# Attention and two feed-forward networks on one core: ten of sixteen probability transfers issued from GpSimd instead of eight, and another order of ten steps of the second network

## The chip, the cores and the metric

The kernel runs on one core of a Trainium2 chip. The metric is the device time of one execution in microseconds; the time before is a median of three runs.

## The reference, cut to what matters

Attention comes first, over 4 batches, 8 heads, 576 positions and 64 dimensions a head. The scores get a bias that a small network makes from the positions:

```python
scores = scale * np.matmul(q, k.transpose(0, 1, 3, 2))
...
h = np.maximum(x @ w1 + b1, 0.0)          # x: log distance of the pair of positions, over log position
bias = h @ w2
attn = np.exp(scores + bias - max) / (sum + 1e-09)
attn_out = attn @ v                        # 2304 tokens x 512
x = (sigmoid(x @ w_gate) * (x @ w_val)) @ moe_w_out        # 512 -> 1536 -> 512
h = x @ w_in                                               # 512 -> 2048
out = (h * clip(h + 3, 0, 6) / 6) @ moe2_w_out             # 2048 -> 512
```

Everything is in 32-bit floats. The kernel keeps that accuracy by splitting each operand of the large products into a high and a low part and multiplying three times (high by high, high by low, low by high).

## The kernel before, in words

**Blocks.** The 576 positions are cut into five chunks: four of 128 and one of 64 (`QC`). A chunk of all four batches is 512 tokens (256 in the last). Chunk 0 gets its attention in a lead-in. Then come five blocks: block k runs both feed-forward networks on chunk k, and between the steps of the networks the attention of chunk k + 1. Blocks begin in the profile at about 81, 311, 557, 783 and 987 us.

**Steps.** The networks of a block are 68 steps, listed by `moe_steps` (line 41). Each takes one weight tile of 512x128 and makes one 128-row product: 24 steps G and V (gate and value), 12 steps Y (first network's output, three for each of four output tiles o), then 16 steps H (second network's hidden tiles) and 16 steps O (its output). Eight O steps, groups g of 0 and 1, stand after the tenth H; the last eight, groups 2 and 3, stand at the end, positions 60 to 67: for each o first g = 2, then g = 3. Group g reads the hidden tiles 4g to 4g + 3, so g = 3 needs the last H (position 59).

**One step.** `product` (line 644) issues twelve matmuls: for each of four input tiles c, three products of high and low parts. They add up in one PSUM bank, `ps`. Then ScalarE and VectorE take the bank: after an H the lines 704, 705, 676 and 678 (clip, product, high part `gh`, low part `gl`), after the last Y of an o the lines 676 and 680 (`xyh`, `xyl`, the inputs of the H steps), after the last O line 720 and the store of line 729. In the last block, of 256 columns, the Y and O steps with o below 3 are "wide": eight matmuls of line 655 in place of twelve, and two more instructions afterwards (670, 671).

**Banks.** The small products draw on a pool of four PSUM banks, `mm_ps`: each step's `ps`, the two tails of `pair_qk` (line 510), the output of `pair_av` (line 567), and the bias products of line 171 that are made "apart".

**Attention between the steps.** `block_events` gives each piece of attention a position on the scale of the 68 steps, and `block` runs all pieces that are due ahead of a step. In blocks 1 to 3 a pair of units goes through `pair_qk` (scores, line 524), `pair_soft` (minimum, exponential, normalisation), `att_turn` (VectorE transposes in 32x32 blocks into the tile `t`, line 446) and `pair_turn` (line 451): sixteen transfers of 72 KB from `t` to `pT`, which finish the transposition. `pair_av` (line 477) multiplies `pT` by the values. `t` and `pT` have one buffer each: the transfers of a pair wait until `pair_av` of the pair before has read `pT`, and the transposes of the next pair wait until all sixteen have read `t`. In block 1 a pair is due every 5.1 steps, in block 2 every 8.1. The sixteen transfers are issued from two queues (lines 454 to 459):

```python
        for i in range(4):
            for q in range(4):
                (nc.sync if p[0][0] < 4 and i > 1 else nc.gpsimd).dma_start(
```

**Order of the work.** TensorE's order is the program's in all blocks. In blocks 1 to 4 the order of the instructions on VectorE, ScalarE, GpSimd and SyncE is laid out by a planner, which works from its own costs of the instructions. Weight tiles come from HBM, five steps ahead, into six buffers (`w_load`, line 586), from SyncE. A queue's instructions run in order.

Of the kernel before, what the change touches and what calls it, by code (L numbers as in the profile page):

```python
# [36 lines left out]
YG, OG = 3, 2  # L37
# [3 lines left out]
def moe_steps():  # L41

    seq = []
    for f in range(NF1):
        seq += [("G", f), ("V", f)]
    for o in range(4):
        seq += [("Y", g, o) for g in range(NF1 // 4)]
    for f in range(NF2):
        seq += [("H", f)]
        if f == NF2 // 2 + 1:  # L50
            seq += [("O", g, o) for o in range(4) for g in range(2)]
    seq += [("O", g, o) for o in range(4) for g in range(2, 4)]
    return seq


STEPS = moe_steps()
NSTEP = len(STEPS)
assert NSTEP == 3 * NF1 + 2 * NF2
# [3 lines left out]
def fused_kernel(ctx: ExitStack, tc: tile.TileContext, qd, kd, vd, tz, td, cst, iden, wpack, out):  # L62
    nc = tc.nc
# [21 lines left out]
    def mm_ps():  # L85
        return m1.tile([128, 512], F32, name="ps")
# [22 lines left out]
    ps = mm_ps()  # L109
# [6 lines left out]
    ps = mm_ps()  # L116
# [334 lines left out]
    def pair_turn(p):  # L451

        t, pt = tn_q.pop(0), A["pt"].tile([128, 4, 2, 9, 32], F32, name="pT")
        for i in range(4):
            for q in range(4):
                (nc.sync if p[0][0] < 4 and i > 1 else nc.gpsimd).dma_start(  # L456
                    out=pt[32 * q:32 * q + 32, i].rearrange("j u t i -> j (u t i)"),
                    in_=t[32 * i:32 * i + 32, q].rearrange("j u t i -> j (u t i)"),
                )
        for x, u in enumerate(p):  # L460
            st[u]["pt"] = pt[:, :, x]
# [89 lines left out]
    def pair_soft(p, x):  # L551
        u = p[x]
        d = st[u]
        ps, m = d.pop("ps"), d["m"]
        for h in range(2):
            pair_min(u, h, ps[:, h, 0:NT], 0, NT, m[:, h:h + 1], 2 + h)
        d["m"] = m[:, 2:4]
        att_exp(u)
        att_norm(u)
        if u[0] == 1:  # L560
            return
        att_turn(p, x)
        if x:
            pair_turn(p)
# [8 lines left out]
    wq, wf_q = {}, {}  # L573
# [67 lines left out]

    ys, gs, accs, th_q, ps_q = {}, {}, {}, {}, {}

    def product(n, nt, ops, mm_ps, first=True, last=True, wide=False):
        wp = wq.pop(n)
        wh, wl = wp[:, 0], wp[:, 1]
        if first:
            ps_q[0] = mm_ps()
        ps = ps_q[0]
        for c in range(4):  # L650
            xh, xl, *both = ops[c]
            if wide:
                pair = [(wh, both[0], ps[:, 0:2 * nt]), (wl, xh, ps[:, 0:nt])]
                for w, x, o in pair if c == 0 else pair[::-1]:
                    nc.tensor.matmul(  # L655
                        out=o, lhsT=w[:, c, :], rhs=x,
                        start=(first and c == 0 and w is wh), stop=(last and c == 3 and w is wh),
                    )
                continue
            for i, (w, x) in enumerate(((wh, xh), (wh, xl), (wl, xh))):  # L660
                nc.tensor.matmul(  # L661
                    out=ps[:, 0:nt], lhsT=w[:, c, :], rhs=x[:, 0:nt],
                    start=(first and c == 0 and i == 0), stop=(last and c == 3 and i == 2),
                )
        return whole(ps, nt) if wide and last else ps[:, 0:nt]

    def whole(ps, nt):

        lo = P["tmp"].tile([128, NTOK], F32, name="tmp")[:, 0:nt]
        nc.scalar.activation(out=lo, in_=ps[:, nt:2 * nt], func=AF.Copy)  # L670
        nc.vector.tensor_tensor(out=lo, in0=ps[:, 0:nt], in1=lo, op=ALU.add)
        return lo

    def split(p, nt, src, scale, nh, nl):
        hi, lo, *both = pair_tiles(p, nt, nh, nl)
        nc.scalar.activation(out=hi, in_=src, func=AF.Copy, scale=scale)  # L676
        if scale == 1.0:
            nc.vector.tensor_tensor(out=lo, in0=src, in1=hi.bitcast(F32), op=ALU.subtract)  # L678
        else:
            nc.vector.scalar_tensor_tensor(  # L680
                out=lo, in0=src, scalar=scale, in1=hi.bitcast(F32), op0=ALU.mult, op1=ALU.subtract
            )
        return hi, lo, *both

    def moe_step(k, i, P, mm_ps):
        n = k * NSTEP + i
        kind = STEPS[i]
        i0, qn = QC[k]
        nt = B * qn
        wide = 2 * nt <= NTOK  # L690
        if kind[0] in "GV":
            ps = product(n, nt, [xs[k, c] for c in range(4)], mm_ps, wide=wide)
            if kind[0] == "G":
                th = ps if wide else P["tmp"].tile([128, NTOK], F32, name="tmp")[:, 0:nt]
                nc.scalar.activation(out=th, in_=ps, func=AF.Tanh, scale=0.5)
                th_q[0] = th
            else:
                th = th_q.pop(0)
                nc.vector.scalar_tensor_tensor(out=th, in0=th, scalar=1.0, in1=ps, op0=ALU.add, op1=ALU.mult)  # L699
                gs[kind[1]] = split(P["gu"], nt, th, 1.0, "gh", "gl")  # L700
        elif kind[0] == "H":
            ps = product(n, nt, [ys[c] for c in range(4)], mm_ps)
            t = P["tmp"].tile([128, NTOK], F32, name="tmp")[:, 0:nt]
            nc.scalar.activation(out=t, in_=ps, func=AF.Relu, bias=3.0)  # L704
            nc.vector.scalar_tensor_tensor(out=t, in0=t, scalar=6.0, in1=ps, op0=ALU.min, op1=ALU.mult)  # L705
            gs[kind[1]] = split(P["gu"], nt, t, 1.0, "gh", "gl")
        elif kind[0] == "Y":
            _, g, o = kind
            ps = product(n, nt, [gs[4 * g + c] for c in range(4)], mm_ps, g == 0, g == YG - 1, wide and o < 3)
            if g == YG - 1:  # L710
                ys[o] = split(xy_p, nt, ps, 0.5, "xyh", "xyl")
        else:
            _, g, o = kind
            ps = product(n, nt, [gs[4 * g + c] for c in range(4)], mm_ps, g % OG == 0, g % OG == OG - 1, wide and o < 3)
            if g == OG - 1:
                accs[o] = P["acc"].tile([128, NTOK], F32, name="acc")[:, 0:nt]
                nc.scalar.activation(out=accs[o], in_=ps, func=AF.Copy, scale=1.0 / 6.0)
            elif g == 2 * OG - 1:
                a = accs.pop(o)
                nc.vector.scalar_tensor_tensor(  # L720
                    out=a, in0=ps, scalar=1.0 / 6.0, in1=a, op0=ALU.mult, op1=ALU.add
                )
                av = a.rearrange("p (b i) -> p b i", b=B)
                for ih in range(NH):
                    lo, hi = max(i0, ih * NI), min(i0 + qn, ih * NI + NI)
                    if lo < hi:
                        for x in range(2):
                            q = nc.gpsimd if k + 1 < NC else (nc.sync, nc.scalar)[x]
                            q.dma_start(  # L729
                                out=out[2 * ih + x, o, :, :, lo - ih * NI:hi - ih * NI],  # L730
                                in_=av[:, 2 * x:2 * x + 2, lo - i0:hi - i0],
                            )
# [242 lines left out]
    def block(k):  # L975
        ev = block_events(k)
        for i in range(NSTEP):
            while ev and ev[0][0] <= i:
                ev.pop(0)[1]()
            if k == 0 and i == NSTEP - 6:  # L980
                held.extend((issued[1], issued[2]))
            n = k * NSTEP + i
            if k == 0:
                if 10 <= n + WA + 1 < NSTEP:
                    w_load(n + WA + 1)
                for x in range(WB - 1 if i == 0 else WB, WB + 1):
                    w_store(n + x - 1)
                    w_split(n + x)
                if i == 0:
                    for last in issued[1], issued[2]:  # L990
                        ctx.enter_context(tc.issue_after(last.ins))
            if n + WA >= NSTEP:
                w_load(n + WA)
            moe_step(k, i, P, mm_ps)
        for e in ev:
            e[1]()
# [72 lines left out]
```

## Time and profile before

| | |
|---|---|
| median of 3 runs | 1091.34 us (1090.79 to 1093.15) |
| the profiled execution | 1092.8 us, its span 1091.0 us |
| TensorE (PE) busy | 99% of the span, 7042 matmuls |
| VectorE (DVE), ScalarE (ACT), GpSimd (POOL) busy | 59%, 49%, 12% |
| granted TensorE clock | 0.999 |
| DMA | 321.94 MB, mean 295 GB/s |

The profile is one execution. A row of the timeline is: start, duration, engine, line, operation, what it writes and reads, how many; in brackets, the idle time of the engine just before it and what ended that.

### The profile page before, as it was taken

The page shows a single profiled execution, that of the slowest core. Times are in us where ns is not written, and L with a number is a line of the kernel's source. Part 1 is how long each engine was busy: PE and PEld are TensorE (multiplying, and loading weights), DVE is VectorE, ACT ScalarE, POOL GpSimd, SP SyncE. Part 2 cuts the span into 40 slices and gives each one's busy share as a digit, 9 for nine tenths or more (in the row PEclk, how much of TensorE's full clock was granted, in tenths as well). Part 3 has the DMA queues.
Part 4 walks back from the last instruction along what each step waited for, and adds up shares of the span by engine and source line. Part 5 has one row for each costly group of instructions (what it writes and reads, how often), then busy time and mean ns, then how long its engine had stood idle before and what let it go on. Part 6 is the DMA issues. An engine that isn't in the chain of part 4 may idle for free.

```text
span 1091.0 us, 19679 instructions
## 1 busy us (share of the span) xinstructions
PE 1079.8 (99%) x7042; PEld 878.7 (81%) x7042; DVE 644.2 (59%) x1528; ACT 537.3 (49%) x1068; POOL 132.3 (12%) x253
## 2 busy tenths in 40 slices
PE   8999999999999999999999999999999999999998
PEld 4777788888887778788788788788788888888897
DVE  8888787797863457796745654656242416154433
ACT  8888688788953344564423342533032214223332
POOL 2000000000010011121311111111430202031000
PEclk9999999999999999999999999999999999999999
DMA  7977899999996789989998888797896969688997
GB/s 244 379 262 289 318 410 368 351 343 403 335 362 229 247 284 291 299 269 284 314 337 262 273 262 270 239 287 249 274 292 213 298 209 278 215 250 308 372 368 266
DMA packets 118480, 321.94 MB, mean 295 GB/s; under 512 B 20720, under 2 KB 29424, under 8 KB 118384
## 3 DMA queue, kind: packets, MB, share of 16 engines
q1 hardware_dynamic: 107968, 297.09, 78.6%
q0 software_dynamic: 9184, 23.25, 7.7%
q8 instruction: 56, 0.92, 0.3%
q10 hardware_dynamic: 1232, 0.35, 0.1%
q14 instruction: 40, 0.33, 0.1%
HBM read 245.08 MB, written 51.37 MB: 272 GB/s over the span
## 4 chain that ended last, share of the span: by engine, by line
PE 82%; ACT 7%; DMA 6%; DVE 3%; issue 2%; SPq 0%; POOL 0%; ACTq 0%; DVEq 0%; POOLq 0%
PE ps L661 59%; PE ps L477 7%; PE ps L655 6%; PE ps L524 3%; PE ps L359 2%; PE ps L416 2%; DMA wd<-wpack 1%; DMA wsp<-wp 1%; PE ps L171 1%; DMA vt<-vd 1%; ACT wp L603 1%; ACT s L390 1%; ACT z L156 1%; PE ps L179 1%; PE ps L530 1%
## 5 line engine op out<-in xcount | busy, mean ns | idle before, releaser
L661 PE MATMUL ps<-xyh,wp 128*128 128x512 f32 (+1 forms) x1472 | 428.7, 378 | 1.1 <-ACT wp L603 0.8
L661 PEld LDWEIGHTS ps<-xyh,wp 128*128 128x128 f32 x1472 | 263.3, 188 | 59.9 <-issue 2.8
L661 PE MATMUL ps<-gh,wp 128*128 128x512 f32 (+1 forms) x980 | 294.7, 383 | 0.5 <-ACT gh L676 0.5
L661 PE MATMUL ps<-xyl,wp 128*128 128x512 f32 x640 | 249.5, 390 | 0.3 <-DVE xyl L680 0.3
L661 PEld LDWEIGHTS ps<-gh,wp 128*128 128x128 f32 x980 | 178.7, 188 | 38.7 <-issue 3.1
L661 PE MATMUL ps<-gl,wp 128*128 128x512 f32 x448 | 174.8, 390 | 0.8 <-DVE gl L678 0.8
L456 POOL DMA_DIRECT2D pT<-t x192 | 94.4, 500 | 493.0 <-DVE t L446 152.8
L676 ACT ACTIVATE gh<-tmp 128x512 fp32r<-128x512 f32 (+1 forms) x140 | 82.1, 588 | 127.4 <-DVE tmp L699 84.0
L661 PEld LDWEIGHTS ps<-xyl,wp 128*128 128x128 f32 x640 | 120.2, 188 | 24.7 <-DVE xyl L680 0.8
L390 ACT ACTIVATE s<-s,m 128x576 f32<-128x576 f32 x144 | 110.3, 768 | 34.5 <-DVE m L546 34.0
L678 DVE TENSOR_TENSOR gl<-tmp,gh 128x512 fp32r<-128x512 f32 x112 | 76.5, 687 | 39.4 <-ACT gh L676 38.4
L661 PEld LDWEIGHTS ps<-gl,wp 128*128 128x128 f32 x448 | 84.1, 188 | 18.7 <-DVE gl L678 2.1
L477 PEld LDWEIGHTS ps<-pT,vt 128*64 128x64 f32 x1600 | 79.0, 137 | 13.0 <-issue 10.9
L477 PE MATMUL ps<-pT,vt 128*64 128x128 f32 (+1 forms) x1600 | 89.1, 265 | 0.1
L705 DVE SCALAR_TENSOR_TENSOR tmp<-tmp,ps 128x512 f32<-128x512 f32 (+1 forms) x80 | 50.0, 629 | 53.6 <-ACT tmp L704 52.2
L699 DVE SCALAR_TENSOR_TENSOR tmp<-tmp,ps 128x512 f32<-128x512 f32 x48 | 32.7, 682 | 74.2 <-PE ps L661 73.4
L704 ACT ACTIVATE tmp<-ps 128x512 f32<-128x512 f32 (+1 forms) x80 | 43.9, 549 | 43.4 <-PE ps L661 43.3
L403 DVE TENSOR_SCALAR s<-s,r 128x576 f32<-128x576 f32 x128 | 61.4, 516 | 1.7
L502 ACT ACTIVATE xyh<-ps 128x256 fp32r<-128x256 f32 (+1 forms) x44 | 15.2, 345 | 95.0 <-PE ps L477 94.8
L729 POOL DMA_DIRECT2D outT<-acc x40 | 27.7, 751 | 261.3 <-DVE acc L720 238.9
L446 DVE STREAM_TRANSPOSE t<-s 128x1152 f32<-128x1152 f32 x40 | 54.3, 1370 | 5.3 <-DMA pT<-t 3.4
L546 DVE CUSTOM_DVE_ANT_0 s<-ps,bm,m 128x320 f32<-128x320 f32 x112 | 56.4, 546 | 0.0
(114 smaller groups left out, 1160.6 us busy)
## 6 DMA issues: line engine op xcount, KB each, us to landing
wp<-wsp SPq DMA_DIRECT2D x272, 512.0 KB, 5.3
wsp<-wp SPq DMA_DIRECT2D x68, 512.0 KB, 6.9
wd<-wpack SPq DMA_DIRECT2D x68, 511.8 KB, 6.4
vt<-vd SPq DMA_DIRECT2D x80, 320.0 KB, 5.5
kt<-kd SPq DMA_DIRECT2D x80, 288.0 KB, 5.8
pT<-t POOLq DMA_DIRECT2D x192, 72.0 KB, 5.6
pT<-t SPq DMA_DIRECT2D x128, 72.0 KB, 4.9
bm<-biasD SPq DMA_DIRECT2D x15, 576.0 KB, 6.4
```

The lines of the kernel that those rows point to most:

```text
L390: nc.scalar.activation(out=s[:, h], in_=s[:, h], func=AF.Exp, scale=-1.0, bias=d["m"][:, h:h + 1], accum_out=r[:, h:h + 1],)
L403: nc.vector.tensor_scalar(out=s[:, h], in0=s[:, h], scalar1=r[:, h:h + 1], scalar2=None, op0=ALU.mult)
L446: nc.vector.transpose(out=tn_q[0][:, :, x], in_=st[u]["s"].rearrange("p h j -> p (h j)").rearrange("p (t q j) -> p q t j", q=4, j=32),)
L456: (nc.sync if p[0][0] < 4 and i > 1 else nc.gpsimd).dma_start(out=pt[32 * q:32 * q + 32, i].rearrange("j u t i -> j (u t i)"), in_=t[32 * ...
L477: nc.tensor.matmul(out=po[64 * h:64 * h + 64, n * a:n * a + n], lhsT=vt[:, v], rhs=pt[:, m * a:m * a + m, k, :], start=(t == 0), stop=(t = ...
L546: nc.vector.tensor_tensor_reduce(out=d["s"][:, h, j0:j1], in0=x, in1=bm_q[c, hp][:, h, j0:j1], scale=-(D ** -0.5), scalar=top, op0=ALU.add ...
L655: nc.tensor.matmul(out=o, lhsT=w[:, c, :], rhs=x, start=(first and c == 0 and w is wh), stop=(last and c == 3 and w is wh),)
L661: nc.tensor.matmul(out=ps[:, 0:nt], lhsT=w[:, c, :], rhs=x[:, 0:nt], start=(first and c == 0 and i == 0), stop=(last and c == 3 and i == 2),)
L676: nc.scalar.activation(out=hi, in_=src, func=AF.Copy, scale=scale)
L678: nc.vector.tensor_tensor(out=lo, in0=src, in1=hi.bitcast(F32), op=ALU.subtract)
L704: nc.scalar.activation(out=t, in_=ps, func=AF.Relu, bias=3.0)
L705: nc.vector.scalar_tensor_tensor(out=t, in0=t, scalar=6.0, in1=ps, op0=ALU.min, op1=ALU.mult)
```

## The change

Three things change. `pair_turn` issues the transfers 0 to 9 of a pair from GpSimd and 10 to 15 from SyncE, in place of 0 to 7 and 8 to 15; the pairs of the last chunk still issue all sixteen from GpSimd. The last eight O steps go in two halves: both g = 2 steps of outputs 0 and 1, then both g = 3 steps, then the same for outputs 2 and 3. And the first two H steps run as one: the first three input tiles of H 0, the first three of H 1, the last of H 0; the last of H 1 stays at its own position. For that, `product` keeps one open bank per key, and can do part of the input tiles.

```diff
-    seq += [("O", g, o) for o in range(4) for g in range(2, 4)]
+    seq += [("O", g, o) for p in (0, 2) for g in range(2, 4) for o in (p, p + 1)]
...
-                (nc.sync if p[0][0] < 4 and i > 1 else nc.gpsimd).dma_start(
+                (nc.sync if p[0][0] < 4 and 4 * i + q > 9 else nc.gpsimd).dma_start(
...
-    def product(n, nt, ops, mm_ps, first=True, last=True, wide=False):
-        wp = wq.pop(n)
+    def product(n, nt, ops, mm_ps, first=True, last=True, wide=False, key=None, cs=range(4)):
+        wp = wq[n]
         wh, wl = wp[:, 0], wp[:, 1]
-        if first:
-            ps_q[0] = mm_ps()
-        ps = ps_q[0]
-        for c in range(4):
+        if first and cs[0] == 0:
+            ps_q[key] = mm_ps()
+        ps = ps_q[key]
+        for c in cs:
...
+        if cs[-1] == 3:
+            del wq[n]
...
         elif kind[0] == "H":
-            ps = product(n, nt, [ys[c] for c in range(4)], mm_ps)
+            f = kind[1]
+            if f == 0:
+                for x in range(2):
+                    product(n + x, nt, ys, mm_ps, key=x, cs=range(3))
+            ps = product(n, nt, ys, mm_ps, key=f, cs=range(3 if f < 2 else 0, 4))
...
-            ps = product(n, nt, [gs[4 * g + c] for c in range(4)], mm_ps, g % OG == 0, g % OG == OG - 1, wide and o < 3)
+            ps = product(n, nt, [gs[4 * g + c] for c in range(4)], mm_ps, g % OG == 0, g % OG == OG - 1, wide and o < 3, key=o)
```

## Rows read from the trace of the kernel before

**Rows 1.** Engines in blocks 0, 1 and 2: stretch, its length, busy time of PE, PEld, DVE, ACT, POOL, clock, DMA share, GB/s.
```profile
81.20:311.00 229.80, 228.43 (x1455) 187.18 (x1454) 182.98 (x410) 190.50 (x349) 3.55 (x6) 1.00 0.94 351
311.00:557.50 246.50, 245.06 (x1509) 194.64 (x1505) 150.38 (x353) 107.13 (x206) 39.78 (x76) 1.00 0.87 284
557.50:782.70 225.20, 224.86 (x1393) 184.13 (x1393) 123.36 (x300) 82.50 (x160) 37.05 (x72) 1.00 0.84 273
```
**Rows 2.** Timeline of PE and DVE, end of block 1.
```profile
530.05 0.39 PE L661 MATMUL ps<-gh,wp 128*128 128x512 f32 x1
...
531.80 2.64 DVE L446 STREAM_TRANSPOSE t<-s 128x1152 f32<-128x1152 f32 x2 [0.91 <-DMA pT<-t]
...
535.07 0.50 PE L661 MATMUL ps<-gl,wp 128*128 128x512 f32 x1 [0.55 <-DVE gl L678]
...
536.30 0.69 DVE L678 TENSOR_TENSOR gl<-tmp,gh 128x512 fp32r<-128x512 f32 x1 [0.69 <-ACT gh L676]
536.33 0.50 PE L661 MATMUL ps<-gh,wp 128*128 128x512 f32 x1 [0.52 <-ACT gh L676]
537.05 0.50 PE L661 MATMUL ps<-gl,wp 128*128 128x512 f32 x1 [0.23 <-DVE gl L678]
```
**Rows 3.** Timeline of PE in block 2, at its first H step.
```profile
679.87 0.39 PE L661 MATMUL ps<-xyh,wp 128*128 128x512 f32 x1
...
682.64 0.50 PE L661 MATMUL ps<-xyl,wp 128*128 128x512 f32 x1 [0.34 <-DVE xyl L680]
...
683.30 0.94 PE L179 MATMUL ps<-z,cst_t 128*32 128x288 f32 x12
```
**Rows 4.** The chain that ended last, in order of time: start, length, what.
```profile
537.93 2.40 PE ps L477 x40
540.34 0.99 PE ps L171 x8
541.33 13.83 PE ps L661 x60
...
1083.66 2.89 PE ps L661 x24
```
**Rows 5.** Timeline of SyncE's queue, GpSimd and DVE around one pair of block 1.
```profile
500.20 9.69 SPq L456 DMA_DIRECT2D pT<-t  x8
...
500.46 3.91 POOL L456 DMA_DIRECT2D pT<-t  x8 [14.84 <-DMA wp<-wsp]
...
512.39 2.64 DVE L446 STREAM_TRANSPOSE t<-s 128x1152 f32<-128x1152 f32 x2 [2.46 <-DMA pT<-t]
```
**Rows 6.** Waits of SyncE's queue, 495 to 535 us: total, times, longest.
```profile
SPq L456 <- DMA wp<-wsp: 8.8, 6, 2.7
```
**Rows 7.** Timeline of GpSimd in block 3, a pair with all sixteen transfers.
```profile
856.07 4.02 POOL L456 DMA_DIRECT2D pT<-t  x8 [44.74 <-DVE t L446]
863.40 0.50 POOL L456 DMA_DIRECT2D pT<-t  x1 [3.31 <-DMA pT<-t]
```
**Rows 8.** DMA issues around 500.5, 509.4 and 863 to 866: count, KB, us to landing.
```profile
pT<-t POOLq DMA_DIRECT2D x1, 72.0 KB, 8.5
...
pT<-t SPq DMA_DIRECT2D x1, 72.0 KB, 2.5
...
pT<-t POOLq DMA_DIRECT2D x4, 72.0 KB, 6.2
```
**Rows 9.** Timeline of DVE and PE in block 1, between H 0 and H 1.
```profile
444.00 0.42 DVE L503 TENSOR_TENSOR xyl<-ps,xyh 128x256 fp32r<-128x256 f32 x1
444.35 0.39 PE L524 MATMUL ps<-kh,qh 64*128 64x256 f32 x2
```
**Rows 10.** DMA issue of one weight tile, 1035.1 to 1035.3 us.
```profile
wp<-wsp SPq DMA_DIRECT2D x1, 512.0 KB, 6.8
```
**Rows 11.** The end: timeline of ScalarE's queue, and its stores' time to landing.
```profile
1085.09 2.52 ACTq L729 DMA_DIRECT2D outT<-acc  x2
...
outT<-acc ACTq DMA_DIRECT2D x4, 64.0 KB, 2.3
```

## The prediction

> **What bounds the kernel now.** I read the busy times by block first, because what the change touches recurs once a block. The reader is to see how little TensorE idles: 229.80 less 228.43 is 1.37 us in block 0, 1.44 in block 1, 0.34 in block 2 [rows 1]. ScalarE and VectorE are busy 83% and 80% of block 0, but 43% and 61% of block 1; TensorE's own work sets the time, and a change of order can win only what TensorE loses in waits.
>
> Then I looked in the timeline for each idle piece. Those of block 1 lie together: 0.55, 0.52 and 0.23 us, 1.30 in all, ahead of matmuls of the O step at the old position 61 (g = 3, o = 0), which waits for the hidden tiles 14 and 15 [rows 2]. These were late because VectorE sat 0.91 us waiting for a pair's transfers, then made two transposes, 2.64 us together, and only then the low parts. Block 2's piece is in the first H step: 0.34 us for the low part of the last Y [rows 3].
>
> The idle pieces aren't the whole loss, since a matmul's row goes on after the next could have begun. The stretch tells more. The two O steps, 24 matmuls, took from 530.05 [rows 2] to 537.93 [rows 4], 7.88 us; undisturbed, 60 matmuls take 13.83 [rows 4], 0.2305 each, so 24 take 5.53. The loss is 2.35 us, not 1.30. The first H step of block 2 took from 679.87 to 683.30 [rows 3], 3.43 us where twelve matmuls take 2.77: a loss of 0.66, of which I count 0.60, as the matmul after it is of another kind and starts a little later anyway. The Trainium skill, "Trainium Kernel Development and Optimization", section "Performance Expectations", says that the busy time of matmuls is a bad measure, because they are pipelined. The trace agrees: by busy time the sum below would be -1.09 us and the change would not be measurable; by the stretches it is -2.40.
>
> **Order of the last eight O steps.** Before, one step (twelve matmuls) stood between the last H and the first g = 3 step. After, there are two, 5.53 us. In block 1, moreover, an attention product (2.40 us) and a bias product (0.99) are due between positions 61 and 62 [rows 4], and now stand ahead of the first g = 3 step. That step would begin at 530.05 + 5.53 + 3.39 = 538.97 and ask for tile 15 nine matmuls later, at 541.0. The tile is ready at 536.30 + 0.69 = 537.0 [rows 2]: a margin of 4.0 us. **Term: -2.35**; the other bound is 0, if something else is late there.
>
> **First two H steps.** Three input tiles of H 1 go in front of H 0's last: nine matmuls, 2.07 us of cover against a loss of 0.6. **Term: -0.60**, other bound 0. Three things pay for it:
>
> - H 1's bank stays open over the attention that stands between positions 36 and 37. In block 1 that is the attention product, a bias product and the two tails of the next scores: with H 1's, five banks wanted of four. So the second tail must take the attention product's bank once VectorE has emptied it. VectorE ended that at 444.42, and the scores began at 444.35 [rows 9]: 0.07 late, plus the signal. I take **+0.10**; bounds 0 and 2.6, should the planner put two transposes [rows 2] ahead of that instruction. Behind it on VectorE then wait low parts of H tiles. It happens once.
> - H 1's weights are wanted nine matmuls after H 0's start instead of twelve. In block 4, where 24 matmuls take 2.89 us [rows 4], that is 0.36 us sooner. A weight tile took 6.8 us to land near there [rows 10], asked for five steps ahead, 5 x 1.44 = 7.2. The margin was 0.4 and is now nil: **+0.05**, bounds 0 and 0.4. Elsewhere five steps are 13.8 us.
> - H 0 ends nine matmuls later, so ScalarE gets H 0 and H 1 close together. In block 0, where it is 83% busy, it may lose up to 2.07 us of ready work; I take 0, because TensorE lost only 1.37 us in all of that block. Of those I count none as gain, since its order changes from the first H on only.
>
> **The end.** In block 4 the new order puts output 2's g = 3 step one step before the end instead of two. Its store leaves at 1085.09 + 1.44 = 1086.5; output 3's, the second of the two issues in those 2.52 us, left at about 1087.0 [rows 11]. An issue occupies the queue for about half a microsecond, so the last store goes 0.1 us late. A store takes 2.3 us to land [rows 11]: moved strictly one after the other, it would be 1.8 late. I take **+0.40**, nearer the low end, as the issues stay half a microsecond apart.
>
> **Two transfers from SyncE to GpSimd.** In block 1 SyncE takes 9.69 us to issue a pair's eight, GpSimd 3.91 [rows 5]. SyncE's issues aren't slow: six times they waited for an earlier weight load to land [rows 6]. Two fewer shorten SyncE's part by 2.4 us (1.2 each), and its next loads start sooner. But GpSimd has such a limit too: where it issues sixteen, eight go out in a row, and the ninth waits until the first may have landed, 7.3 us after the first went [rows 7]. In block 1 the first took 8.5 us to land [rows 8], so the ninth would leave at 508.96 and the tenth at 509.5. SyncE's eighth, issued at 509.4, landed after 2.5 [rows 8]. If the tenth takes as long, the pair is complete at 512.0 instead of 511.9: one limit of eight has been exchanged for another. If it takes 6.2, as late ones on GpSimd's queue did in block 3 [rows 8], it is complete at 515.7, 3.8 late. I take the 2.5, a row of the same moment and load: **term 0**, bounds -0.5 (the pair complete sooner by a transfer's issue, and felt by TensorE) and +3.8 a pair. VectorE already waits 2.46 us at that place, with no idle piece of TensorE's [rows 5]. In block 2, with 8.1 steps a pair, these microseconds have cover.
>
> **The sum.** -2.35 - 0.60 + 0.10 + 0.05 + 0.40 + 0 = -2.40 us. The profiled execution took 1092.8 us, 1.8 of them around its span; it would take 1090.4. The median of the runs is 1.46 lower than the profiled one: from 1091.34 the sum leads to 1088.94. I forecast **1089.0 us**, 0.21% less. A measurement of this kernel can tell about 0.2% (2.2 us, here 1089.16) from no change: the forecast lies just beyond that line, and what is left of the gain decides on which side it falls.
>
> **Rivals.**
>
> *Part of the gain is given back (1090.3).* If the loss is only what the idle pieces show, the sum is -1.30 - 0.34 + 0.55 = -1.09. The same comes out if the planner, which lays out VectorE and ScalarE anew in blocks 1 to 4, puts a low part behind transposes at one other step, at some 1.3 us. For it: both losses had a low part late on VectorE [rows 2, 3]. Against it: there were two such in three blocks, and the stretches measure the loss directly.
>
> *Nothing moves (1091.3).* The losses come back in full elsewhere, -2.95 + 2.95, or the last store costs its 1.8 and the open bank its worst.
>
> *GpSimd's ninth and tenth transfers become the bound (1094.0, slower).* Place: pairs of block 1. Price: 3.8 us late, as much as 3.8 on TensorE where nothing absorbs it; at two pairs 7.6, of which I leave a third to VectorE's and the banks' slack, so +5.1; less the gains of 2.4, +2.7. It decides from about 2 us of lateness on, since waits of that size have been free. For it: 6.2 us in block 3. Against it: 2.5 at the very moment, and 4.0 us of margin at the end of the block. That the two transfers move nothing at all is the forecast's own term.
>
> **Chances.** The forecast's case 0.52, part given back 0.24, nothing moves 0.12, GpSimd's limit 0.12. The forecast's case spreads about a microsecond to either side (the runs before lie from 0.55 below their median to 1.8 above), so some 0.44 of it is beyond 0.2% and 0.08 within. Faster 0.44, same 0.08 + 0.24 + 0.12 = 0.44, slower 0.12. The range goes from 1087.9 (the bounds of the end and the bank at their lower ends, -2.85, and the spread of 0.55) to 1092.2 (nothing won, and the runs a little high): outside lie the slower rival and the edges of the others. The likeliest case's own range is 1087.9 to 1090.0.
>
> **What would show it.** Right: the two g = 2 steps ending block 1 in 5.5 us and the g = 3 steps behind them with no idle piece; none at the first H of block 2; in block 1 eight transfers from GpSimd in a row, a wait for a landing, then two more; SyncE's issue time there down by about a quarter; the last stores half a microsecond apart. Wrong: VectorE's waits for transfers in block 1 past 4 us, with idle pieces of TensorE behind them; an idle piece at the scores after H 0 in block 1; more than 2 us of idle time in block 0; or the last store over a microsecond later behind the last matmul.

## The result and the profile after

The changed kernel took 1098.33 us (median of 12 runs, 1092.14 to 1101.04), the kernel before beside it 1090.69 (12 runs, 1089.95 to 1093.15): a ratio of 1.0061, interval 1.0047 to 1.0075. It is slower by 0.6%; the forecast was 1089.0. Ratios and intervals here and below are worked out from the times of all executions in the fast state, not from the two medians (whose quotient is 1.0070 for this pair).

The windows of the changed kernel by block (columns as in [rows 1], blocks 0 to 2):

```profile
81.20:311.00 229.80, 229.37 (x1462) 188.41 (x1461) 183.44 (x411) 191.20 (x351) 3.55 (x6) 1.00 0.94 352
311.00:557.50 246.50, 245.24 (x1508) 195.52 (x1507) 150.12 (x353) 106.75 (x206) 48.05 (x93) 1.00 0.88 290
557.50:782.70 225.20, 217.65 (x1326) 178.78 (x1325) 122.16 (x298) 82.14 (x159) 42.91 (x85) 0.99 0.81 256
```

Block 2 stands out: TensorE idles 225.20 - 217.65 = 7.55 us there, where it idled 0.34 [rows 1]. The list of TensorE's waits (total, times, longest) names the instruction:

```profile
PE ps L477 <- DMA wp<-wsp: 6.6, 3, 2.7
...
PE ps L477 <- DVE gl L680: 1.0, 1, 1.0
PE ps L524 <- DVE tmp L711: 0.9, 1, 0.9
...
PE ps L524 <- DVE xyl L503: 0.4, 1, 0.4
```

L477 is the attention product, and it reads no `wp`. The list puts a wait down to whatever ended last before it; here that is a weight tile that was landing beside the pair's last transfers, and in the fourth wait VectorE, long done. Both hide a wait for `pT`, as the landings below show.

Landmarks put a size on each block: the first attention product of block 1, of block 2 and of block 3 in TensorE's timeline, before and then after, and the last row of the chain after (before: [rows 4]).

```profile
422.18 1.09 PE L477 MATMUL ps<-pT,vt 128*64 128x128 f32 x15
...
586.89 1.31 PE L477 MATMUL ps<-pT,vt 128*64 128x128 f32 x20
...
842.39 0.80 PE L477 MATMUL ps<-pT,vt 128*64 128x64 f32 x20
```

```profile
420.75 0.98 PE L477 MATMUL ps<-pT,vt 128*64 128x128 f32 x14
...
585.17 1.09 PE L477 MATMUL ps<-pT,vt 128*64 128x128 f32 x16
...
849.50 0.69 PE L477 MATMUL ps<-pT,vt 128*64 128x64 f32 x16
```

```profile
1092.26 1.45 PE ps L661 x12
```

The changed kernel is 1.43 us ahead at the start of block 1, 1.72 at the start of block 2, 7.11 behind at the start of block 3, and the last matmul ends 7.16 later (1093.71 against 1086.55). Block 2 cost 8.83 us. The 1.43 of block 0 is no gain of the order: the second experiment below, with the old order, starts its first product at 420.89 too.

The end of block 1 and the first H step of block 2, in TensorE's timeline, answer to [rows 2, 3]:

```profile
530.67 0.39 PE L661 MATMUL ps<-gh,wp 128*128 128x512 f32 x1
...
536.20 2.40 PE L477 MATMUL ps<-pT,vt 128*64 128x128 f32 x40
...
539.53 0.50 PE L661 MATMUL ps<-gh,wp 128*128 128x512 f32 x1
...
682.23 0.39 PE L661 MATMUL ps<-xyh,wp 128*128 128x512 f32 x1
...
687.08 1.18 PE L179 MATMUL ps<-z,cst_t 128*32 128x288 f32 x16
```

The two g = 2 steps take 536.20 - 530.67 = 5.53 us, as worked out, and the next step starts at 539.53 without an idle piece. The 21 matmuls of H 0 and H 1 take 4.85, 0.231 each. Both old losses are gone.

Where block 2 lost: its second pair, in the timelines of SyncE's queue, GpSimd and TensorE, then the landings (count, KB, us to landing) of GpSimd's first transfer, SyncE's first weight tile and GpSimd's last two transfers.

```profile
600.24 3.71 SPq L456 DMA_DIRECT2D pT<-t  x6
...
600.77 4.90 POOL L456 DMA_DIRECT2D pT<-t  x10 [21.54 <-DMA wp<-wsp]
...
604.05 2.19 SPq L586 DMA_DIRECT2D wp<-wsp  x3
...
613.17 0.66 PE L477 MATMUL ps<-pT,vt 128*64 128x128 f32 x8 [1.84 <-DMA wp<-wsp]
```

```profile
pT<-t POOLq DMA_DIRECT2D x1, 72.0 KB, 1.9
...
wp<-wsp SPq DMA_DIRECT2D x1, 512.0 KB, 6.5
...
pT<-t POOLq DMA_DIRECT2D x2, 72.0 KB, 7.7
```

GpSimd issues all ten in a row. Its first lands after 1.9 us, its last two, issued 0.6 and 1.1 us behind the first weight tile, after 7.7 on the mean of the two. The tenth landed at 613.09, and the product started at 613.17, 1.84 us idle before it.

The fourth pair shows the other delay, the one that the prediction had in its rival:

```profile
656.36 4.03 POOL L456 DMA_DIRECT2D pT<-t  x8 [23.48 <-DVE t L446]
665.00 0.50 POOL L456 DMA_DIRECT2D pT<-t  x1 [4.62 <-DMA pT<-t]
...
672.54 0.66 PE L477 MATMUL ps<-pT,vt 128*64 128x128 f32 x8 [2.07 <-DMA wp<-wsp]
```

Eight, a wait of 4.62 us until the first has landed, then the ninth. The trace's semaphores say whose limit this is: GpSimd's transfers report their landings on eight of them in turn (111 to 118), the first and the ninth of this pair share 114, and the ninth waits for it. So the eight is this program's; whether a queue has a limit of its own no run here shows.

Four products of block 2 lose time: at 613.17, 672.54, 729.76 and 758.58. The other four start 0.32 us after the start of the matmul ahead of them; these start later than that by 1.91, 2.14, 2.73 and 1.04 us, 7.8 in all. Behind the third, the longest, the granted clock fell:

```profile
730.00:735.00 5.00, 5.00 (x58) 4.83 (x56) 0.64 (x2) 0.39 (x1) 0.00 (x0) 0.66 0.33 113
```

A clock of 0.66 over 5 us means that TensorE ran part of it at the lower of its two levels, 1.2 GHz, and lost 5 x 0.34 = 1.7 us. 7.55 - 0.34 of idle time and 1.7 of clock are 8.9 us, which accounts for the 8.83.

### The profile page after: what moved, and what is told of

The parts are those of the page before. It is cut to its first block, busy times and chain, and to the rows that moved or that the text cites. A ratio compares the mean times of both kernels' runs of the same rounds, so it can differ in the third digit from the quotient of the medians.

```text
span 1098.2 us, 19661 instructions
## 1 busy us (share of the span) xinstructions
PE 1081.2 (98%) x7042; PEld 881.8 (80%) x7042; DVE 643.7 (59%) x1528; ACT 537.2 (49%) x1068; POOL 148.7 (14%) x285
## 4 chain that ended last, share of the span: by engine, by line
PE 83%; DMA 8%; ACT 5%; DVE 3%; issue 2%; SPq 0%; POOL 0%; ACTq 0%; DVEq 0%; POOLq 0%
PE ps L661 59%; PE ps L477 7%; PE ps L655 6%; PE ps L524 3%; DMA wp<-wsp 2%; PE ps L359 2%; PE ps L416 2%; PE ps L171 1%; DMA pT<-t 1%; DMA wd<-wpack 1%; DMA biasD<-bo 1%; PE ps L432 1%; DMA qt<-qd 1%; DMA wsp<-wp 1%; PE ps L530 1%
## 5 line engine op out<-in xcount | busy, mean ns | idle before, releaser
L456 POOL DMA_DIRECT2D pT<-t x224 | 110.7, 501 | 503.0 <-DVE t L446 200.4
L477 PE MATMUL ps<-pT,vt 128*64 128x128 f32 (+1 forms) x1600 | 90.8, 268 | 7.5 <-DMA wp<-wsp 6.6
L477 PEld LDWEIGHTS ps<-pT,vt 128*64 128x64 f32 x1600 | 80.7, 139 | 20.5 <-issue 16.7
L711 DVE SCALAR_TENSOR_TENSOR tmp<-tmp,ps 128x512 f32<-128x512 f32 (+1 forms) x80 | 50.0, 628 | 59.0 <-ACT tmp L710 57.7
L502 ACT ACTIVATE xyh<-ps 128x256 fp32r<-128x256 f32 (+1 forms) x44 | 15.2, 345 | 103.9 <-PE ps L477 103.8
L623 DVE SCALAR_TENSOR_TENSOR wp<-wd,wp 128x512 fp32r<-128x512 f32 x68 | 46.7, 689 | 16.6 <-ACT wp L603 15.8
```

The costliest lines, as they stand in the source:

```text
L456: (nc.sync if p[0][0] < 4 and 4 * i + q > 9 else nc.gpsimd).dma_start(out=pt[32 * q:32 * q + 32, i].rearrange("j u t i -> j (u t i)"), in_ ...
L477: nc.tensor.matmul(out=po[64 * h:64 * h + 64, n * a:n * a + n], lhsT=vt[:, v], rhs=pt[:, m * a:m * a + m, k, :], start=(t == 0), stop=(t = ...
L623: nc.vector.scalar_tensor_tensor(out=wv[:, 1], in0=cm_q.pop(n).bitcast(F32), scalar=256.0, in1=wv[:, 0].bitcast(F32), op0=ALU.mult, op1=AL ...
```

## The experiments

Each ratio is to the kernel before run beside it. O is the new order of the last eight steps, H the interleaving of the first two H steps; a division is GpSimd/SyncE transfers a pair; the idle columns are TensorE's in the windows of [rows 1], in us, from the profiled execution.

| | O | H | block 1 | block 2 | median (runs), us | range, us | ratio to before | idle bl. 1 | idle bl. 2 |
|---|---|---|---|---|---|---|---|---|---|
| before | no | no | 8/8 | 8/8 | 1090.69 (12) | 1089.95-1093.15 | 1 | 1.44 | 0.34 |
| after | yes | yes | 10/6 | 10/6 | 1098.33 (12) | 1092.14-1101.04 | 1.0061 [1.0047, 1.0075] | 1.26 | 7.55 |
| 1 | yes | yes | 8/8 | 8/8 | 1093.46 (12) | 1088.06-1096.37 | 1.0017 [1.0002, 1.0033] | 3.83 | 1.32 |
| 2 | no | no | 10/6 | 10/6 | 1096.33 (5) | 1093.45-1098.94 | 1.0055 [1.0043, 1.0068] | 0.48 | 3.59 |
| 3 | yes | yes | 10/6 | 8/8 | 1091.35 (11) | 1089.87-1093.24 | 1.0005 [0.9997, 1.0014] | 2.16 | 0 |
| 4 | yes | yes | 8/8 | 10/6 | 1097.57 (8) | 1092.43-1106.59 | 1.0076 [1.0043, 1.0108] | 0 | 3.65 |
| 5 | yes | yes | 10/6+2 | 10/6+2 | 1094.08 (12) | 1091.07-1097.24 | 1.0027 [1.0015, 1.0039] | 1.17 | 1.56 |
| 6 | yes | yes | 10/6 | 6/10 | 1091.35 (12) | 1089.97-1093.30 | 1.0002 [0.9993, 1.0011] | 1.68 | 0 |
| 7 | yes | no | 8/8 | 8/8 | 1089.66 (12) | 1088.30-1090.98 | 0.9983 [0.9975, 0.9992] | 0 | 1.10 |
| 8 | no | yes | 8/8 | 8/8 | 1100.05 (6) | 1095.80-1102.79 | 1.0085 [1.0067, 1.0103] | 1.59 | 1.86 |
| 9 | yes | yes | 8/6/2 | 8/6/2 | 1095.67 (5) | 1094.98-1096.94 | 1.0046 [1.0033, 1.0059] | 6.36 | 0.18 |
| 10 | yes | no | 8/8 | 6/10 | 1088.99 (11) | 1088.16-1089.58 | 0.9982 [0.9973, 0.9991] | 0 | 0.30 |
| 11 | yes | no | 6/10 | 6/10 | 1096.95 (6) | 1093.68-1102.03 | 1.0062 [1.0044, 1.0081] | 4.53 | 2.82 |
| 12 | yes | no | 10/6 | 6/10 | 1088.54 (6) | 1088.00-1089.43 | 0.9970 [0.9958, 0.9982] | 0 | 0.30 |
| 13 | no | yes | 10/6 | 6/10 | 1093.03 (12) | 1090.32-1095.84 | 1.0013 [1.0001, 1.0024] | 3.08 | 0 |
| 14 | no | yes | 8/8 | 8/8 | 1098.63 (1) | | | 3.89 | 1.23 |

One execution of the twelfth took 3789 us. It is left out of the range and the ratio, but counted in the median; that of the other five is 1088.31. The profiled executions of the second (1093.45 us), the fourth (1092.43) and the eighth (1095.80) were the fastest of their runs, so their idle columns are small beside their medians. What the slower ones lost, up to 1106.59 in the fourth, was not profiled.

### 1 to 4: which part, and in which block

The division is the condition in the transfer's line; O and H are the parts of the diff above. The first takes back the division, the second has the division alone, the third has it in block 1 alone, as here, the fourth with `== 3` in block 2 alone:

```diff
-(nc.sync if p[0][0] < 4 and 4 * i + q > 9 else nc.gpsimd)
+(nc.sync if p[0][0] < 4 and 4 * i + q > (9 if p[0][0] == 2 else 7) else nc.gpsimd)
```

Order alone:

> This kernel has the new order of the O and H steps and the old eight and eight transfers. Theory T (the loss is made by the transfers: in block 2 the last three that GpSimd issues land behind weight loads that SyncE now sends earlier, and the attention product waits for them): the new order alone wins what the prediction summed for it, so about 1088.5 us, 0.2% less than before, and no wait of TensorE at the attention products of block 2. Rival R (the loss comes from the new order: five banks wanted of four, and another order of VectorE's and ScalarE's work): about 1095 to 1098 us, with the idle pieces still there.

Transfers alone:

> This kernel has the ten and six transfers and the old order of steps. Theory T: slower than the changed kernel or like it, 1096 to 1101 us, with waits of 1 to 3 us at several attention products of block 2, and the old loss of 2.35 us at the end of block 1 still there. Rival R: about 1090 to 1091 us, like before.

Ten in block 1 alone:

> New order of steps; ten and six transfers in the pairs of block 1 only, eight and eight in block 2. Theory T: the waits of block 2 go; about 1089 to 1091 us, what is left being the two waits of block 1 (1.2 and 0.8 us) at the scores. Rival R: 1095 to 1098 us.

Ten in block 2 alone:

> New order of steps; eight and eight transfers in block 1, ten and six in the pairs of block 2 only. Theory T: nearly all of the loss is there, 1095 to 1098 us, with the four waits of block 2 of 1 to 3 us. Rival R: also 1095 to 1098 us; a second rival, by which the loss starts in block 1 and is only handed on, gives about 1089 to 1090 us.

The third and fourth kernel's windows of blocks 1 and 2, one after the other:

```profile
311.00:557.50 246.50, 244.34 (x1504) 194.79 (x1503) 149.96 (x353) 106.58 (x205) 47.86 (x92) 1.00 0.88 289
557.50:782.70 225.20, 225.20 (x1397) 184.83 (x1396) 123.35 (x300) 82.49 (x160) 39.01 (x75) 1.00 0.85 269
```

```profile
311.00:557.50 246.50, 246.50 (x1517) 196.78 (x1516) 151.06 (x354) 107.22 (x207) 40.05 (x77) 1.00 0.89 293
557.50:782.70 225.20, 221.55 (x1380) 181.77 (x1379) 122.31 (x299) 82.39 (x160) 45.77 (x90) 1.00 0.83 263
```

The loss is made by ten transfers in block 2: with them there block 2 idles 3.6 us and the median is near that of the changed kernel, without them it idles nothing. In block 1 ten do no harm.

Two expectations missed. The old loss at the end of block 1 was to stay in the second kernel; there the two O steps take 6.37 us, where [rows 2] and [rows 4] gave 7.88 and an undisturbed pair of steps takes 5.53:

```profile
528.75 0.39 PE L661 MATMUL ps<-gh,wp 128*128 128x512 f32 x1
...
535.12 2.15 PE L477 MATMUL ps<-pT,vt 128*64 128x128 f32 x35
```

So ten from GpSimd in block 1 take back 1.5 of the 2.35 us with the old order of steps, and the two changes don't add. And the first kernel doesn't win what the order was to win (1093.46, not 1088.5), and its runs spread over 8 us; that needed the runs from the seventh on.

### 5 and 9: why the last two of ten are late

The fifth lets SyncE issue two spare transfers behind its six; the ninth gives two of GpSimd's ten to ScalarE's queue.

```diff
+        for x in range(2 if p[0][0] < 4 else 0):
+            nc.sync.dma_start(out=spare[x], in_=t[96:128, 2 + x].rearrange("j u t i -> j (u t i)"))
```

```diff
-(nc.sync if p[0][0] < 4 and 4 * i + q > 9 else nc.gpsimd)
+(nc.sync if p[0][0] < 4 and 4 * i + q > 9 else nc.scalar if p[0][0] < 4 and 4 * i + q > 7 else nc.gpsimd)
```

> This is the changed kernel, but behind its six transfers of a pair SyncE issues two spare ones of the same size into a DRAM scratch buffer that nothing reads, so that its weight loads are again issued behind eight transfers, as in the kernel before (some 144 KB more a pair are moved). Theory passing (SyncE's 512 KB weight loads, issued two transfers sooner, land ahead of GpSimd's last two or three transfers and push them back): the last transfers of block 2's pairs land some 2 to 4 us sooner than in the changed kernel, the attention products of block 2 lose under 2 us together instead of 7.6, and the median is 1090 to 1093. Rival limit (GpSimd's ninth and tenth transfer wait until its first has landed, whatever SyncE does): the losses of block 2 stay at 4 to 8 us, median 1095 to 1099. Rival traffic (the 16 engines are full, and it is the sum of bytes that counts): more bytes, more loss, 1099 or more.

> The changed kernel with its new step order and its six transfers from SyncE, but in blocks 1 and 2 GpSimd issues eight instead of ten and ScalarE the other two. SyncE's weight loads start as early as in the changed kernel. Theory late issue (what costs is that GpSimd's ninth and tenth transfer are issued last, 4 us or more after the first one, behind SyncE's weight loads; by the trace of the changed kernel they land some 2 to 4 us behind the others): ScalarE issues its two at once, the pair is complete some 2 to 3 us sooner than in the changed kernel, the attention products of block 2 lose under 2 us, median 1090 to 1093. Rival early weights (with only six transfers on SyncE its weight loads take the DMA engines' time from whatever of the pair is under way): the last of GpSimd's eight still land behind the loads, block 2 loses 4 us or more, median 1095 to 1099. Rival ScalarE (a transfer that waits for t holds up ScalarE's own work behind it): matrix products wait for ScalarE's tiles in block 1, median 1094 or more with block 2 whole.

The fifth kernel's second pair of block 2: SyncE's queue, then the landings of GpSimd's last two transfers.

```profile
603.90 1.05 SPq L462 DMA_DIRECT2D spare<-t  x2
605.05 1.34 SPq L589 DMA_DIRECT2D wp<-wsp  x3
```

```profile
pT<-t POOLq DMA_DIRECT2D x2, 72.0 KB, 3.9
```

The weight tiles now go at 605.05, about when GpSimd's tenth goes, and the same two transfers land after 3.9 us on the mean, not 7.7 (the tenth, which completes the pair, after 5.2, not 7.9). At the fourth pair GpSimd still waits 2.93 us for its first landing. Block 2's idle time falls from 7.55 to 1.56, and the median by 4.2 us, of the 7.0 that ten in block 2 cost (third kernel to the changed one), though more bytes move. So the weight tiles' passing ahead is one cause; that GpSimd's late ninth and tenth are the rest is what the ninth kernel tests. The theory that the bytes count is out.

The ninth kernel's windows of blocks 1 and 2:

```profile
311.00:557.50 246.50, 240.14 (x1449) 191.13 (x1448) 149.38 (x351) 105.29 (x205) 37.89 (x74) 0.99 0.85 280
557.50:782.70 225.20, 225.02 (x1396) 184.69 (x1395) 123.22 (x300) 82.50 (x160) 37.60 (x74) 1.00 0.84 271
```

Block 2 is whole with SyncE at six, so its early weights do no harm where nothing of a pair is issued behind them: "late issue" holds. The median is still 1095.67, because block 1 idles 6.36 us: by the list of waits 5.7 us of TensorE's go to VectorE's L503, which takes a tile of ScalarE's L502, and that stands behind the two transfers in ScalarE's order:

```profile
445.12 3.18 ACTq L456 DMA_DIRECT2D pT<-t  x2
...
448.35 0.38 ACT L502 ACTIVATE xyh<-ps 128x256 fp32r<-128x256 f32 x1 [3.59 <-DMA pT<-t]
...
449.34 0.55 PE L524 MATMUL ps<-kh,qh 64*128 64x256 f32 x1 [3.06 <-DVE xyl L503]
```

The third theory holds for block 1.

### 6, 10 and 11: the opposite division

The sixth keeps ten from GpSimd in block 1 and has six in block 2, as here; the tenth, without H, has 7 in place of 9, the eleventh 5 in both blocks:

```diff
+(nc.sync if p[0][0] < 4 and 4 * i + q > (9 if p[0][0] == 2 else 5) else nc.gpsimd)
```

> New step order, ten transfers from GpSimd in block 1 as in the third experiment, and in block 2 the opposite division: six from GpSimd and ten from SyncE. Theory passing: SyncE's weight loads are issued two transfers later than with eight and eight, nothing of a pair stands behind them, and block 2's attention products lose nothing; the weights have some us in hand, so block 2 stays within 0.5 us of its 225.20 and the median is that of the third experiment, 1090.5 to 1092. Rival longest queue (whichever engine issues ten finishes last, at 1.2 us a transfer on SyncE): the pair is complete some 2.4 us later than with eight and eight, products of block 2 lose 2 to 6 us, median 1093 to 1097. Rival weights: matrix products of the steps wait for SyncE's loads, 1 to 3 us in all, median 1092 to 1094.

> Only the other order of the last eight steps (as in the seventh experiment), and in block 2 six transfers from GpSimd and ten from SyncE. The seventh experiment's profile still lost 0.82 us at the block's sixth pair (product started 0.88 us behind the last landing). Theory slack (a pair counts only where its last landing comes behind the product's planned start, and SyncE's ten are complete a little sooner than eight and eight): the sixth pair loses under 0.3 us, median 1088.3 to 1089.6, a little under the seventh experiment. Rival nothing: the same as the seventh, 1089.3 to 1090. Rival weights (SyncE's weight loads come 1.2 us later and a matrix step waits for them): 1090 to 1092.

> As the run before it, with six and ten in block 1 as well. In block 1 the pairs have 6 us and more in hand with eight and eight (the seventh experiment), but SyncE's queue is fuller there (waits of its weight loads of several us). Theory slack: block 1 stays whole, 246.4 to 246.5 us of TensorE's work in 246.50, median within 0.5 us of the run before it, 1088.3 to 1089.8. Rival weights: with two more transfers ahead of them SyncE's weight loads come late at the end of block 1 and steps wait for them, 1 to 3 us, median 1090.5 to 1093.

In block 2 six from GpSimd and ten from SyncE lose nothing: the weights wait behind the pair and have time. The tenth's sixth pair starts without a wait (0.82 us lost in the seventh), but its gain over the seventh, 1088.99 against 1089.66, is within what the intervals leave open. In block 1 the same division costs 8 us (eleventh against tenth). (The 2.82 us that the eleventh idles in block 2's window are 2.53 at the last pair of block 1, whose product falls into it, and 0.3 that the tenth has too.) SyncE's queue at block 1's last two pairs, with ten in the eleventh and with eight in the seventh kernel:

```profile
523.14 13.78 SPq L456 DMA_DIRECT2D pT<-t  x10
...
544.91 14.22 SPq L456 DMA_DIRECT2D pT<-t  x10
```

```profile
517.81 4.96 SPq L456 DMA_DIRECT2D pT<-t  x8
...
536.74 5.17 SPq L456 DMA_DIRECT2D pT<-t  x8
```

Ten take 14 us to issue, eight 5, and six 3.7 (twelfth): from 519 to 562 us the eleventh's issues wait 14.1 us, eight times, for earlier weight loads to land. 1096.95 us lies outside both expectations. It wasn't the weights that came late there, as the rival had it, but the transfers themselves: VectorE's transposes wait 7.93 and 4.51 us for them, and TensorE for VectorE.

### 7, 8, 12, 13 and 14: the two orders apart

The seventh is the diff's O line on the kernel before (with a bank per output), the eighth the diff without that line and without the transfers' line; the twelfth and thirteenth are these with 10/6 in block 1 and 6/10 in block 2; the fourteenth is the eighth once more.

> Eight and eight transfers, the old interplay of the first two steps of the second network, and only the other order of the last eight steps of a chunk. Theory first steps (what keeps the new order of the first experiment from its gain, and makes its runs differ, is the interleaving of the first two steps: a bank held open, transposes ahead of VectorE's work, two steps' weights wanted at once): this kernel gains the 2.35 us of the end of block 1 and loses nothing, median 1088 to 1089.5, runs within 2 us. Rival last steps (the order of the last eight steps removes the cover that the transfers and weights at the block's end had): median 1092 to 1094, runs from 1088 to 1096.

> Eight and eight transfers, the old order of the last eight steps, and only the interleaving of the first two steps of the second network. Theory first steps: the first steps gain 0.6 us and cost 1 to 3 us behind block 1's scores, median 1091.5 to 1094, runs differ by several us. Rival last steps: median 1090 to 1091, the 0.6 us of block 2's first step gained, runs within 2 us as in the kernel before.

> Only the other order of the last eight steps; ten transfers from GpSimd and six from SyncE in block 1, six and ten in block 2. This is the sixth experiment without the interleaving of the first two steps; that one lost 1.25 and 1.17 us at two scores of block 1 (463 and 483 us). Theory first steps (the interleaving puts transposes ahead of the tile that the scores' first matmul needs): the scores lose nothing, block 1 has 246.3 us or more of TensorE's work in 246.50, median 1088.3 to 1089.6. Rival ten in block 1 (the loss comes with GpSimd's ten, which change VectorE's order too): block 1 loses 1 to 2.5 us at its scores, median 1090 to 1091.5.

> Only the interleaving of the first two steps, the old order of the last eight, and ten and six transfers in block 1, six and ten in block 2: the eighth experiment with SyncE's queue relieved in block 1 and GpSimd's in block 2. Theory queue (the interleaving by itself costs 1 to 3 us at most; the rest of the 9 us of the eighth experiment comes from SyncE's transfers backing up, 9 to 12 us from issue to landing at the end of block 1 and at block 2's sixth pair): median 1091 to 1094, SyncE's transfers of probabilities land within 6 us in block 2. Rival steps (the interleaving itself costs the 9 us, whatever the transfers do): median 1097 or more.

> The kernel of the eighth experiment once more, for a second profile: its profiled execution took 1095.8 us, the others 1099 to 1103. Theory queue: an execution of 1099 us or more shows further waits for SyncE's transfers (landings of 9 us and more) at the end of block 1 or in block 2, and a lower granted clock behind them. Rival: the time goes in other places, in block 3 or 4 or in many small losses without a wait.

O without H is faster than before with three divisions (7, 10, 12) and slower with six and ten in block 1 (11). H costs time in each of the three pairs of kernels that differ in it alone: 1 against 7, 6 against 12, 8 against before, 3.8, 2.8 and 9 us. For the eighth neither expectation came near (1091.5 to 1094, 1090 to 1091).

Where O gains, in the seventh kernel's first products of block 1 and of block 2:

```profile
420.89 2.40 PE L477 MATMUL ps<-pT,vt 128*64 128x128 f32 x40
...
583.26 2.40 PE L477 MATMUL ps<-pT,vt 128*64 128x128 f32 x40
```

From one to the other it takes 162.37 us, the kernel before 586.89 - 422.18 = 164.71: 2.34 less, the term's 2.35.

Where H costs: VectorE and TensorE at the scores of the second pair behind H 0, in the changed kernel and in the twelfth.

```profile
459.87 2.64 DVE L446 STREAM_TRANSPOSE t<-s 128x1152 f32<-128x1152 f32 x2
462.43 0.65 DVE L711 SCALAR_TENSOR_TENSOR tmp<-tmp,ps 128x512 f32<-128x512 f32 x1
...
463.13 0.38 PE L524 MATMUL ps<-kh,qh 64*128 64x256 f32 x1 [0.87 <-DVE tmp L711]
```

```profile
456.97 2.64 DVE L446 STREAM_TRANSPOSE t<-s 128x1152 f32<-128x1152 f32 x2
...
461.45 0.39 PE L524 MATMUL ps<-kh,qh 64*128 64x256 f32 x2
```

With H, two transposes stand ahead of the instruction (L711) that empties the bank which the second tail's scores want; TensorE loses 1.24 us there. Without H the transposes come 2.5 us earlier, measured from the attention product ahead of the scores (458.66 and 458.22), and both tails start together. The thirteenth has 1.25 and 1.71 us of the same, and the granted clock is 0.91 over 480 to 500 us behind the second; the queue theory is right for it in so far as block 2 is whole, SyncE's transfers land there within 5.7 us, and 7 of the 9 us are gone. In the fourteenth, VectorE's transposes wait for a pair's transfers, and an O step at the end of block 1 waits for VectorE:

```profile
535.22 2.64 DVE L446 STREAM_TRANSPOSE t<-s 128x1152 f32<-128x1152 f32 x2 [2.76 <-DMA pT<-t]
...
538.48 0.50 PE L661 MATMUL ps<-gl,wp 128*128 128x512 f32 x1 [3.37 <-DVE gl L680]
```

That is the wait of [rows 2], 0.55 us before, now 3.37, because VectorE waits 2.76 us for the transfers where it waited 0.91; the clock is 0.92 over the 20 us behind it, and block 2's sixth pair loses 1.30 us. Why H makes SyncE's transfers back up at the end of block 1 (eight took 11.33 and 9.48 us to issue in the eighth kernel, 4.96 and 5.17 in the seventh) is not settled: VectorE's and SyncE's order change with it, and nothing was run that changes one of them alone.

## Why the prediction was wrong

**The step that failed** is the term 0 for the two transfers, and in it the sentence "In block 2, with 8.1 steps a pair, these microseconds have cover." The bounds were worked out for a pair of block 1, and block 2 was passed over because its period is long. But the product of a pair comes two periods behind its scores in block 1 and one behind in block 2. The trace of before held the answer. The landing of the sixth pair's last transfer, issued from SyncE at 720.46, and the product behind it:

```profile
pT<-t SPq DMA_DIRECT2D x1, 72.0 KB, 4.0
```

```profile
725.36 1.86 PE L477 MATMUL ps<-pT,vt 128*64 128x128 f32 x30
```

720.46 + 3.99 = 724.45: 0.91 us of margin; at three other pairs of block 2 it was 3.1, at the rest 5 to 7. With ten on GpSimd the last landing comes 2 to 7 us later (11 to 16 us behind the first issue, before 7 to 10), and four of eight pairs run out of margin: the second, fourth, sixth and seventh pair take 4.9, 6.6, 3.5 and 3.9 us longer, less their margins of 3.1, 4.9, 0.9 and 3.1 that is 1.8, 1.6, 2.6 and 0.8, and TensorE idled 1.84, 2.07, 2.67 and 0.97 there. The 0.91 wasn't even free with eight and eight: in the seventh kernel the same product idles 0.75 us and starts 0.88 behind its last landing (721.66, 722.54), in the changed kernel 0.09. The term measured 7.0 us in medians where block 1 has ten (third experiment to the changed kernel), 4.1 where it has eight (first to fourth), and 5.6 for both blocks on the kernel before (second).

**The slower rival** had the mechanism half right (the ninth waits for a landing: 4.62 us at the pair shown) and the place wrong. In block 1 the pairs kept 2.5 us or more. SyncE's issue at the priced pair fell from 9.69 us for eight to 3.7 for six, by more than the quarter worked out: before, its issues waited for weight loads, after, they didn't, and that doesn't go in equal parts of 1.2 us. The other half, SyncE's weight tiles passing ahead of GpSimd's last two, was listed as a benefit ("its next loads start sooner"). The Trainium skill, "DMA: Bandwidth & Descriptors", section "Issuing engines are not separate DMA queues", says that transfers from all issuing engines run on the same 16 DMA engines and interleave, so that another issuer saves only sequencer time. The landings after 7.7 us behind the weight tiles and 3.9 beside them agree.

**The O order, -2.35: right where nothing else changes.** Alone it gains 1.9 us [0.9, 2.7] (7), and 2.34 between the two products in the profile; with another division as well, 2.0 [1.0, 2.9] (10) and 3.3 [2.0, 4.6] (12). The stretch was the right measure: the idle pieces were only 1.30. But the sum added it to the transfers' term as if they were independent, and ten in block 1 by themselves had already taken 1.5 of it (second).

**The H order, -0.60 and +0.10: the gain right, the cost in the wrong place.** The gain is there: from the first product of block 2 to the first of block 3 the sixth kernel takes 254.78 us (585.85 to 840.63), the tenth, which has the same division in block 2 and no H, 255.36 (582.39 to 837.75), 0.58 more. The open bank cost nothing where it was priced: between positions 36 and 37 the scores start 3.23 us behind the product in the changed kernel (441.74, 444.97), 3.22 in the kernel before (441.13, 444.35). The cost stands at the next two pairs, 1.24 and 0.76 us in the changed kernel, 1.25 and 1.71 in the thirteenth, where H 1's bank is no longer open: VectorE's transposes stand ahead of the instruction that empties a bank. That is close to what the rival "part of the gain is given back" expected of the planner's new order, at one place and 1.3 us; it came at two. Together the two terms had the wrong sign.

**The end, +0.40: nothing.** From the last matmul to the end of the span it is 1091.0 - 1086.55 = 4.5 us before and 1098.2 - 1093.71 = 4.5 after. **Block 0** neither gained nor lost by the order, as said. The +0.05 for weights in block 4 is nothing in the changed kernel; the fourteenth waits 0.17 us for H 1's tile there (1047.65), nine matmuls behind the start of H 0, by the way that the term names. (The low end of the range adds up to -2.90, not -2.85, which leaves it at 1087.9.)

The version with the lowest median is the twelfth: O alone, ten from GpSimd in block 1 and ten from SyncE in block 2, 0.3% faster than before. That its division adds to O isn't shown: the intervals of the seventh and tenth, 0.2% faster, overlap with it.

## What to carry to other kernels

Before moving a transfer, list for every consumer in the kernel how long before its start the last transfer lands, and price the move at the smallest of these margins, not at the block where the queue is fullest. Two queues of one kernel can want opposite divisions in two stages: here ten from SyncE cost 8 us in block 1 and nothing in block 2, ten from GpSimd nothing in block 1 and 4 to 7 us in block 2. A queue relieved of work sends its next transfers sooner; ask whose tail they overtake.

## What was not expected of the hardware

- A wait of TensorE's can cost more than itself: behind 2.67 us without a matmul the granted clock of the changed kernel was 0.50, the lower level, from 730.00 to 733.40. It fell as well behind 3.37 us in the fourteenth and behind 0.41 and 1.34 us close together in the thirteenth (483.69 and 485.41), but not behind 2.07 in the changed kernel or 2.19 in the second, so that the length of a wait alone doesn't tell. In the changed kernel's runs the granted clock over the span goes from 1.000 (1092.14 us) to 0.996 (1101.04); 0.4% of 1101 us is 4.4 us, by this estimate at most half of what lies between these two, since the span's clock counts the stretch behind the last matmul too.
- Executions of one kernel spread by 14.2 us in the fourth experiment and 8.3 in the first, whose profiles show products waiting for their pair, and by 1.4 in the tenth and the twelfth, where no pair of blocks 1 and 2 has less than 1.4 us in hand. That the waits make the spread isn't shown: the thirteenth has no such wait in its profile and spreads by 5.5.
